# A recurrent-attention and MLP kernel on one core: a planner's order is replaced by a written one, with fewer activation-table changes and half of the transposes done by DMA

## The chip, the cores and the metric

The kernel runs on one core of a Trainium2 chip. The metric is the device time of one execution in microseconds (us); of several runs the median counts. A profile gives the span, from the first to the last instruction of one execution, and what each engine did in it: PE (TensorE matmuls; PEld its weight loads), DVE (VectorE), ACT (ScalarE), POOL (GpSimd), SP (SyncE, here only an issuer of DMAs).

## What is computed

A gated linear recurrence over 768 steps for 4 batches and 8 heads of 48 channels, then an MLP with SiLU on all 3072 tokens:

```python
f = 1.0 / (1.0 + np.exp(-f_logit))
for t in range(S):                                        # S = 768
    state = f[:, :, t, :, None] * state + np.einsum('bhd,bhe->bhde', k[:, :, t], v[:, :, t])
    y[:, :, t] = np.einsum('bhd,bhde->bhe', q[:, :, t], state)
x = y.transpose(0, 2, 1, 3).reshape(B * S, H * D)         # 3072 x 384
h = x @ w_in                                              # 384 x 2048
return (h * (1.0 / (1.0 + np.exp(-h)))) @ w_out           # 2048 x 384
```

## The kernel before

The sequence is cut into 6 chunks of 128 steps; a chunk of one batch is a *unit*, 24 in all, and two units of the same chunk make a *pair*, 12 in all. A unit passes these steps, named as in the code:

- Loads of `f`, `k`, `q`, `v` from HBM by SP (L381), in rows of 48 floats (192 bytes). Units 0 to 3 are loaded singly (192 KB per tensor), the others in pairs (384 KB).
- ACT: `E` (L388) and `L` (L390) make log(1 + exp(-f)). PE: `cs` (L431, L435) sums it over the steps. ACT: `ia` (L438) and `a` (L440) are exp of the sum and of its negative, `al` (L442) the decay over the chunk.
- POOL: `ki` = k x `ia` (L444), `vb` = v in bf16 (L446). DVE: `qg` = q x `a` (L448). Both products lie in one tile, `qk`.
- PE: `tq` transposes `qk` in eight matmuls against an identity (L454); DVE: `qkc` copies the result out of PSUM as `qkT` (L456).
- PE: `sc` = scores (L465); DVE: `at` masks them (L469). PE: `y` (L474 with the state of the chunk before, L478 within the chunk). DVE: `yc` copies y to bf16 (L482). PE: `yT` transposes it (L486); DVE: `xc` copies it into `xT` (L488).
- PE: `d` (L494), DVE: `sd` (L499, L501) and POOL: `su` (L505) carry the state on to the next chunk.

A pair then passes the MLP: eight `mi` (L412, six matmuls of 256 columns each), each followed on ACT by `si`, SiLU (L408); for each unit four `mo` (L422, four matmuls of 384 columns each); DVE: `oc` (L425) copies the result out, and `so` (L428) stores it, on POOL's queue but for the last two units. `wi` (L400) and `wo` (L403) load the MLP's weights in four parts each, on POOL's queue.

The order is made by a planner inside the kernel: `make_tasks` gives each step an engine, a duration and a rank, `schedule` plays them against numbers of buffers (`SLOTS`) and a model of the two DMA queues, and the tasks are emitted in order of their planned start. Every engine runs its own instructions in exactly that order. On ACT the planner knows two modes, `exp` for E, L, `ia`, `a`, `al` and `silu` for `si`, and adds 1.29 us where the mode turns. The code names one activation table at the start only:

```python
nc.scalar.preload_act_table_set("natural_log_exp_and_others")
```

PSUM is divided by use: `mlp` three banks, `sc` two, `tq` (for `tq` and `yT`), `cs` and `yd` (for `y` and `d`) one each. `CFG["turned"]` says from which unit on `qk` is transposed by a DMA (`qkD`) in place of `tq` and `qkc`; it is 24, so no unit is.

Of the kernel before, what the change touches and what calls it, by code (L numbers as in the profile page):

```python
# [18 lines left out]
CHUNKS, BATCHES = 6, 4  # L19
UNITS = CHUNKS * BATCHES  # L20
PAIRS = UNITS // 2
NTILES = 16

CFG = dict(
    margin=0.35,
    pace=4.43,
    turned=24,
    dma_rate=187.0,
    w_after=(2, 2, 2, 2, 2, 2, 2, 4),
    hold_exp=0.28,  # L30
    hold_silu=0.58,
    keep_exp=166.39,
    keep_silu=46.33,
    rank=dict(ld=-19.78, E=-11.45, cs=-8.27, ia=-3.88, ki=-66.76, vb=-27.12, qg=6.22, tq=-14.46, qkc=71.64,
              sc=-51.69, at=-136.35, y=-13.92, yc=-24.21, yT=-146.22, xc=36.71, d=5.82, sd=-59.94, su=-32.83,
              mi=-43.24, si=-2.57, mo=11.89, mstep=0.05, oc=38.35, so=-26.29, wi=-16.05, wo=-11.92),
)
# [4 lines left out]
LAT = {"PE": 0.25, "ACT": 0.14, "DVE": 0.14, "POOL": 0.08, "SP": 0.0}  # L42
TABLE = 1.29

class Task:
    def __init__(self, name, eng, dur, prio, deps=(), acq=(), use=(), mode=None, phase=None, load=0.0):
        self.name, self.eng, self.dur, self.prio = name, eng, dur, prio
        self.deps, self.acq, self.use = list(deps), list(acq), list(use)
        self.mode, self.phase, self.load = mode, phase, load  # L50

class Inst:
    def __init__(self, key, cls):
        self.key, self.cls = key, cls

def make_tasks(cfg):
    T, tasks, pace, R = {}, [], cfg["pace"], cfg["rank"]

    def add(name, *a, **k):
        t = Task(name, *a, **k)
        T[name] = t
        tasks.append(t)
        return t

    kb = lambda n: n * 1024.0 / (cfg["dma_rate"] * 1e3)
    I = {}

    def inst(key, cls):  # L70
        if key not in I:
            I[key] = Inst(key, cls)
        return I[key]

    base = lambda u: pace * u
    for P in range(PAIRS):
        u0 = 2 * P
        for n, x in enumerate("fkqv"):
            inst((x, P), x)
        groups = [(u0,), (u0 + 1,)] if P < 2 else [(u0, u0 + 1)]  # L80
        for us in groups:
            for n, x in enumerate("fkqv"):
                add((x, us), "SP", 0.35 * len(us), base(us[0]) + R['ld'] + n * 0.1, acq=[I[x, P]], load=kb(192 * len(us)))
    load_of = lambda x, u: T[x, (u,)] if u < 4 else T[x, (u - u % 2, u - u % 2 + 1)]

    for P in range(PAIRS):
        us_list = [(2 * P,), (2 * P + 1,)] if P < 2 else [(2 * P, 2 * P + 1)]
        for us in us_list:
            n = len(us)
            ph = us[0] // 2 - 1 if us[0] >= 4 else 0  # L90
            e = add(("E", us), "ACT", 0.067 + 0.32 * n, base(us[0]) + R['E'], deps=[T["f", us]], acq=[inst(("e", us), "e")],
                    use=[I["f", P]], mode="exp", phase=ph)
            add(("L", us), "ACT", 0.067 + 0.32 * n, base(us[0]) + R['E'] + 0.1, deps=[e], acq=[inst(("lf", P), "lf")],
                use=[I["e", us]], mode="exp", phase=ph)
    log_of = lambda u: T["L", (u,)] if u < 4 else T["L", (u - u % 2, u - u % 2 + 1)]

    for u in range(UNITS):
        c, b, P, B = u // BATCHES, u % BATCHES, u // 2, base(u)
        last, ph = c == CHUNKS - 1, u // 2
        dmat = u >= cfg["turned"]  # L100
        for key in ("cs", "ia", "qk", "vb", "qkT", "atm", "yb", "sc", "al"):
            inst((key, u), key)
        inst(("y", u), "yd"), inst(("d", u), "yd"), inst(("tq", u), "tq"), inst(("yT", u), "tq")
        inst(("sd", u), "sd"), inst(("st", u), f"st{b}"), inst(("xT", P), "xT"), inst(("hT", P), "hT")
        cs = add(("cs", u), "PE", 0.162 + (0 if last else 0.1), B + R["cs"], deps=[log_of(u)], acq=[I["cs", u]], use=[I["lf", P]])
        ia = add(("ia", u), "ACT", 0.387, B + R["ia"], deps=[cs], acq=[I["ia", u]], use=[I["cs", u]], mode="exp", phase=ph)
        a = add(("a", u), "ACT", 0.38, B + R["ia"] + 0.1, deps=[ia], use=[I["cs", u]], mode="exp", phase=ph)
        if not last:
            al = add(("al", u), "ACT", 0.19, B + R["ia"] + 0.2, deps=[cs], acq=[I["al", u]], use=[I["cs", u]], mode="exp", phase=ph)
        ki = add(("ki", u), "POOL", 1.02, B + R["ki"], deps=[ia, load_of("k", u)], acq=[I["qk", u]], use=[I["ia", u], I["k", P]])  # L110
        vb = add(("vb", u), "POOL", 0.62, B + R["vb"], deps=[load_of("v", u)], acq=[I["vb", u]], use=[I["v", P]])
        qg = add(("qg", u), "DVE", 0.45, B + R["qg"], deps=[a, load_of("q", u)], acq=[I["qk", u]], use=[I["cs", u], I["q", P]])
        if dmat:
            qkT = add(("qkD", u), "SP", 2.3, B + R["tq"], deps=[qg, ki], acq=[I["qkT", u]], use=[I["qk", u]], load=0.5)
        else:
            tq = add(("tq", u), "PE", 0.45, B + R["tq"], deps=[qg, ki], acq=[I["tq", u]], use=[I["qk", u]])
            qkT = add(("qkc", u), "DVE", 0.6, B + R["qkc"], deps=[tq], acq=[I["qkT", u]], use=[I["tq", u]])
        sc = add(("sc", u), "PE", 0.41, B + R["sc"], deps=[qkT], acq=[I["sc", u]], use=[I["qkT", u]])
        at = add(("at", u), "DVE", 1.21, B + R["at"], deps=[sc], acq=[I["atm", u]], use=[I["sc", u]])
        yd = [at, vb] + ([T["su", u - BATCHES]] if c else [])  # L120
        y = add(("y", u), "PE", 0.39 if c else 0.22, B + R["y"], deps=yd, acq=[I["y", u]],
                use=[I["atm", u], I["vb", u], I["qkT", u]] + ([I["st", u - BATCHES]] if c else []))
        yc = add(("yc", u), "DVE", 0.47, B + R["yc"], deps=[y], acq=[I["yb", u]], use=[I["y", u]])
        yT = add(("yT", u), "PE", 0.17, B + R["yT"], deps=[yc], acq=[I["yT", u]], use=[I["yb", u]])
        xc = add(("xc", u), "DVE", 0.3, B + R["xc"], deps=[yT], acq=[I["xT", P]], use=[I["yT", u]])
        if not last:
            d = add(("d", u), "PE", 0.17, B + R["d"], deps=[ki, vb, y], acq=[I["d", u]], use=[I["qk", u], I["vb", u]])
            sdd = [d] + ([T["su", u - BATCHES]] if c else [])
            sd = add(("sd", u), "DVE", 0.47, B + R["sd"], deps=sdd, acq=[I["sd", u]],
                     use=[I["d", u]] + ([I["st", u - BATCHES]] if c else []))  # L130
            add(("su", u), "POOL", 0.75, B + R["su"], deps=[sd, al], acq=[I["st", u]], use=[I["sd", u], I["al", u]])

    for n in range(4):
        add(("wi", n), "POOL", 0.8, R["wi"] + n, deps=[T["ki", cfg["w_after"][n]]], load=786.432e3 / 341e3)
    for n in range(4):
        add(("wo", n), "POOL", 0.8, R["wo"] + n, deps=[T["ki", cfg["w_after"][4 + n]]], load=786.432e3 / 341e3)

    for P in range(PAIRS):
        B = base(2 * P + 1)
        for j in range(NTILES // 2):  # L140
            h = inst(("h", P, j), "mlp")
            mi = add(("mi", P, j), "PE", 0.655, B + R["mi"] + j * R["mstep"], deps=[T["xc", 2 * P], T["xc", 2 * P + 1], T["wi", j // 2]],
                     acq=[h], use=[I["xT", P]])
            add(("si", P, j), "ACT", 0.504, B + R["si"] + j * R["mstep"], deps=[mi], acq=[I["hT", P]], use=[h], mode="silu")
        for i in range(2):
            u = 2 * P + i
            o = inst(("o", u), "mlp")
            for m in range(4):
                mo = add(("mo", u, m), "PE", 0.655, B + R["mo"] + (4 * i + m) * R["mstep"],
                         deps=[T["si", P, 2 * m], T["si", P, 2 * m + 1], T["wo", m]] + ([T["mo", u, m - 1]] if m else []),  # L150
                         acq=[o], use=[I["hT", P]])
# [7 lines left out]
def schedule(tasks, slots, cfg, margin=0.0, fixed=None, dur=None):  # L159

    for i, t in enumerate(tasks):
        t.idx, t.start, t.end, t.succ, t.ready, t.left = i, None, None, [], 0.0, len(t.deps)
# [394 lines left out]
```

## Time and profile before

| what | value |
|---|---|
| three runs | 218.91, 221.58, 223.65 us; median 221.58 |
| span of the profiled execution | 217.2 us |
| profiled execution's own time | not listed apart from the three runs; the median is 4.4 us over the span |
| PE, ACT, DVE, POOL busy | 181.0, 149.4, 102.7, 75.0 us |
| mean granted clock of PE | 0.976 |
| DMA | 27.02 MB, 124 GB/s mean; 99,712 of 104,628 packets under 512 bytes |
| activation-table loads on ACT | 38 of 1283 ns |

The page cuts the span into 40 slices of 5.43 us; a digit is the busy share of an engine in tenths, PEclk the clock that PE was granted, GB/s what the DMA engines moved. A group row gives the line, engine, operation, tiles and shapes, the count, the busy time, the mean of one in ns, and the idle time ahead of them with what ended most of it. A stage row gives the stage, its length, and the busy time of PE, PEld, DVE, ACT and POOL with counts, then clock, DMA share (above 1 where transfers overlap) and GB/s. A wait row gives who waited for whom, the total, how often, and the longest. A timeline row gives start, duration, engine, line, operation, tiles and count; SPq rows are SP's queue issuing DMAs. PE's busy time is modelled for pipelined matmuls, so a busy PE need not be a dense one.

The DMA row `GB/s` of the first five slices is 121, 164, 163, 169, 196. DMA issues take, from issue to landing, a median of 5.2 to 5.3 us for 192 KB loads, 7.7 to 8.1 for 384 KB loads, 9.2 (shortest 5.8) for a part of `w_in`, 12.0 (shortest 7.5) for a part of `w_out`, 3.9 for a store from POOL and 1.9 for the last two from SP.

### The profile page before, as it was taken

The page shows a single profiled execution, that of the slowest core. Times are in us where ns is not written, and L with a number is a line of the kernel's source. Part 1 is how long each engine was busy: PE and PEld are TensorE (multiplying, and loading weights), DVE is VectorE, ACT ScalarE, POOL GpSimd, SP SyncE. Part 2 cuts the span into 40 slices and gives each one's busy share as a digit, 9 for nine tenths or more (in the row PEclk, how much of TensorE's full clock was granted, in tenths as well). Part 3 has the DMA queues.
Part 4 walks back from the last instruction along what each step waited for, and adds up shares of the span by engine and source line. Part 5 has one row for each costly group of instructions (what it writes and reads, how often), then busy time and mean ns, then how long its engine had stood idle before and what let it go on. Part 6 is the DMA issues. An engine that isn't in the chain of part 4 may idle for free.

```text
span 217.2 us, 4591 instructions
## 1 busy us (share of the span) xinstructions
PE 181.0 (83%) x1872; PEld 135.4 (62%) x1872; DVE 102.7 (47%) x201; ACT 149.4 (69%) x230; POOL 75.0 (35%) x126
## 2 busy tenths in 40 slices
PE   0366889945999966969969969986999999999992
PEld 0344668624578646648748738754769677786761
DVE  3277730027455526545545446444585573745111
ACT  4444249965079899995999995999845658662440
POOL 2248830042274146144343335235253321510100
PEclk9999999995699999999999999999999999999999
DMA  7999999999999999999999999011001010100101
GB/s 121 164 163 169 196 188 184 178 164 187 174 223 220 164 200 167 197 194 177 179 194 180 163 191 185 4 38 38 3 36 39 0 39 36 39 36 3 41 31 72
DMA packets 104628, 27.02 MB, mean 124 GB/s; under 512 B 99712, under 2 KB 103552, under 8 KB 104608
## 3 DMA queue, kind: packets, MB, share of 16 engines
q1 hardware_dynamic: 99488, 19.27, 70.1%
q0 software_dynamic: 5120, 7.47, 15.1%
q8 instruction: 14, 0.23, 0.5%
q14 instruction: 6, 0.05, 0.1%
HBM read 25.17 MB, written 4.72 MB: 138 GB/s over the span
## 4 chain that ended last, share of the span: by engine, by line
PE 62%; ACT 19%; DMA 6%; SPq 5%; issue 3%; DVE 2%; POOL 0%; DVEq 0%; ACTq 0%; POOLq 0%
PE mlp L412 27%; PE mlp L422 21%; SPq L381 5%; ACT L438 4%; DMA w_out_sb<-in_moe_w_out_dram 3%; PE tq L454 3%; ACT lf L390 3%; PE sc L465 3%; ACT L390 3%; DMA f<-in_f_logit_dram 2%; ACT e L388 2%; ACT L388 2%; ACT ia L438 2%; PE yd L478 2%; PE cs L431 2%
## 5 line engine op out<-in xcount | busy, mean ns | idle before, releaser
L408 ACT ACTIVATE hT<-mlp 128x512 bf16<-128x512 f32 x96 | 56.1, 597 | 28.6 <-PE mlp L412 25.0
L422 PE MATMUL mlp<-w_out_sb,hT 128*128 128x384 bf16 x384 | 71.5, 331 | 2.6 <-DMA w_out_sb<-in_moe_w_out_dram 2.6
L412 PE MATMUL mlp<-xT,w_in_sb 128*128 128x256 bf16 x576 | 68.8, 276 | 3.3 <-DVE o L425 1.7
L412 PEld LDWEIGHTS <-w_in_sb 128*128 128x128 bf16 x576 | 55.8, 99 | 11.5 <-issue 3.6
L422 PEld LDWEIGHTS <-hT 128*128 128x128 bf16 x384 | 35.6, 99 | 23.0 <-issue 3.6
L469 DVE TENSOR_TENSOR atm<-sc,triu 128x512 bf16<-128x512 f32 x48 | 30.9, 685 | 31.0 <-PE sc L465 30.9
L444 POOL TENSOR_TENSOR qk<-k,ia 128x384 bf16<-128x384 f32 x24 | 23.9, 996 | 58.5 <-ACT ia L438 50.4
L448 DVE TENSOR_TENSOR qk<-q,cs 128x384 bf16<-128x384 f32 x24 | 13.2, 550 | 37.5 <-ACT al L442 36.3
L428 POOL DMA_DIRECT2D out_dram<-o x22 | 12.7, 576 | 41.6 <-DVE o L425 36.7
L505 POOL TENSOR_TENSOR st<-sd,al 48x192 bf16<-48x192 f32 x40 | 20.0, 500 | 19.4 <-DVE sd L499 8.2
L438 ACT ACT_TABLE_LOAD x14 | 18.0, 1283 | 9.2 <-PE cs L435 8.6
L454 PE MATMUL tq<-ident,qk 128*128 128x128 bf16 x192 | 16.8, 238 | 8.9 <-DVE xT L488 6.2
L456 DVE COPY qkT<-tq 128x1024 bf16<-128x1024 bf16 x24 | 16.5, 687 | 8.5 <-PE tq L454 8.5
L425 DVE COPY o<-mlp 128x384 f32<-128x384 f32 x24 | 13.2, 552 | 15.0 <-PE mlp L422 14.9
L454 PEld LDWEIGHTS <-qk 128*128 128x128 bf16 x192 | 13.2, 106 | 11.2 <-issue 6.9
L438 ACT ACTIVATE ia<-cs 128x384 f32<-128x384 f32 x24 | 11.7, 490 | 11.6 <-PE cs L435 7.5
L431 PE MATMUL cs<-lf,triu 128*128 128x384 bf16 x24 | 8.4, 350 | 13.2 <-ACT lf L390 7.9
L482 DVE CAST yb<-yd 128x384 bf16<-128x384 f32 x24 | 13.3, 554 | 10.9 <-PE yd L478 10.7
L388 ACT ACTIVATE e<-f 128x768 f32<-128x768 f32 (+1 forms) x14 | 10.5, 748 | 8.0 <-DMA f<-in_f_logit_dram 8.0
L446 POOL CAST vb<-v 128x384 bf16<-128x384 f32 x24 | 11.7, 503 | 10.5 <-issue 5.0
L435 PEld LDWEIGHTS <-lf 128*128 128x128 bf16 x80 | 5.1, 100 | 15.1 <-issue 13.8
L408 ACT ACT_TABLE_LOAD x10 | 12.8, 1283 | 0.2
(35 smaller groups left out, 154.3 us busy)
## 6 DMA issues: line engine op xcount, KB each, us to landing
out_dram<-o POOLq DMA_DIRECT2D x22, 192.0 KB, 3.9
f<-in_f_logit_dram SPq DMA_DIRECT2D x10, 384.0 KB, 8.1
k<-in_k_dram SPq DMA_DIRECT2D x10, 384.0 KB, 7.7
q<-in_q_dram SPq DMA_DIRECT2D x10, 384.0 KB, 7.9
v<-in_v_dram SPq DMA_DIRECT2D x10, 384.0 KB, 7.8
w_in_sb<-in_moe_w_in_dram POOLq DMA_DIRECT2D x4, 384.0 KB, 9.2
w_out_sb<-in_moe_w_out_dram POOLq DMA_DIRECT2D x4, 384.0 KB, 12.0
f<-in_f_logit_dram SPq DMA_DIRECT2D x4, 192.0 KB, 5.2
```

The lines of the kernel that those rows point to most:

```text
L388: nc.scalar.activation(e, at("f", u // 2)[:, i:i + n, :, 0:D], AF.Exp, scale=-1.0)
L408: return nc.scalar.activation(at("hT", P)[:, 2 * j:2 * j + 2, :], h, AF.Silu)
L412: nc.tensor.matmul(h[:, i, :], w_in_sb[:, kk, n * 128:(n + 1) * 128], at("xT", P)[:, kk, :], start=(kk == 0), stop=(kk == KT - 1))
L422: nc.tensor.matmul(o, at("hT", P)[:, n, i * C:(i + 1) * C], w_out_sb[:, n, :], start=(n == 0), stop=(n == NT - 1))
L425: nc.vector.tensor_copy(at("ob", u), at("o", u)[:, 0:d_model])
L438: nc.scalar.activation(at("ia", u).rearrange("p h d -> p (h d)"), at("cs", u)[:, 0:HD], AF.Exp)
L444: nc.gpsimd.tensor_mul(at("qk", u)[:, 1, :, 0:D], at("k", P)[:, i, :, 0:D], at("ia", u))
L454: nc.tensor.transpose(t_ps[:, j, p, :], at("qk", u)[:, j, 2 * p:2 * p + 2, :], ident)
L456: nc.vector.tensor_copy(at("qkT", u), at("tq", u).rearrange("p (j n c) -> p j n c", j=2, c=C))
L469: nc.vector.tensor_mul(at("atm", u)[:, r], at("sc", u)[:, r], triu[:, None, :].to_broadcast([C, NP, C]))
L482: nc.vector.tensor_copy(at("yb", u), at("y", u))
L505: nc.gpsimd.tensor_mul(at("st", u)[lo:lo + D, :, r * D:(r + 1) * D], at("sd", u)[lo:lo + D, :, r * D:(r + 1) * D], at("al", u)[lo:lo + D, ...
```

## The change

The planner goes. `PLAN` is a text with one word for each step, in order: name, pair and unit, engine (P, A, V, G for POOL, S for SP) and buffers. `run` reads a word and calls `emit`, which issues nearly the same instructions as before. What differs:

The built order of ACT has 18 table loads: one at the start and 17 turns. Before it has 38.
- **PSUM.** All eight banks are one pool `pb`, used by `cs`, `tq`, `sc` (two banks), `y`, `yT`, `d`, `h` and `o` as the plan says. `a` goes to a tile in SBUF, no longer in place into `cs`.
- **Turned by DMA.** For pairs 6 to 11 (12 units) `qkD` transposes `qk` straight into `qkT` and `yD` transposes `yb` straight into `xT`, both issued by SP; `tq`, `qkc`, `yT` and `xc` remain for pairs 0 to 5.
- **Idle matmuls.** 79 matmuls of 512 columns (and two of 128) with zeros as data stand in PE's order, in twelve groups, nearly all ahead of the first `mi`.
- **Other engines.** ACT takes 13 `yc`, 13 `oc`, 5 `vb`, 4 `xc`, 4 `sd`, 3 `qkc`; DVE takes 7 `ki` and 7 `vb`; POOL takes 10 `qg`. 11 of 24 stores go through SP.
- **Loads.** `f` comes in 384 KB per pair, `k`, `q`, `v` in 192 KB per unit, each at a place of its own in SP's order. The numbers of buffers change (`f` 4, `v` 6, `vb` 7, `atm` 4, `ob` 6).
- The 16 `mi` of pairs 0 and 1 are split into halves of 128 columns, one for each unit.

`emit` also holds another form of pair ("T"), which no pair uses.

```diff
-SLOTS = dict(f=5, k=6, q=6, v=5, e=2, lf=3, ia=2, qk=5, vb=6, qkT=4, atm=3, yb=3, xT=4, hT=4, sd=2, al=6, o=3,
-             st0=1, st1=1, st2=1, st3=1, mlp=3, sc=1, tq=1, cs=1, yd=1)
+SLOTS = dict(f=4, k=6, q=6, v=6, e=2, lf=3, x=5, qk=5, vb=7, qkT=4, atm=4, yb=3, xT=4, hT=4, sd=2, al=6, ob=6, pb=8, st0=1, st1=1, st2=1, st3=1)
...
+PLAN = """
+f.0.0:S:0 f.1.0:S:1 f.2.0:S:2 E.0.0:A:0 L.0.0:A:0 v.1.1:S:0 idle.512.23::7 cs.0.1:P:0 k.1.1:S:0 cs.0.0:P:1 ia.0.1:A:0 E.1.0:A:1 k.0.1:S:1 q.0.1:S:0
...
+al.1.0:A:1 ia.0.0:A:3 qg.0.0:V:2 k.2.1:S:2 al.2.1:A:2 idle.512.1::6 sc.1.1:P:6,4 vb.1.1:A:2 ki.0.0:G: ia.2.0:A:4 at.1.1.0:V:1 al.0.1:A:3 al.2.0:A:4
+k.2.0:S: wi.0:G: ki.1.0:V:3 idle.512.3::1 tq.0.0:P:7 y.0.1:P:1 qkc.0.0:V:2 d.0.1:P:0 q.2.0:S: yc.0.1:A:0 al.1.1:A:5 at.1.1.1:V: qg.1.0:G: a.2.1:A:2
...
+mo.9.1.0:P:1 si.9.7:A: mo.9.0.0:P:4 qg.11.1:V:2 ki.11.1:V: mo.9.1.1:P: qkD.11.1:S:2 mo.9.0.1:P: oc.7.0:V:0 mi.10.0:P:6 v.11.1:S: mi.10.2:P:0
...
+        elif kind == "qkD":
+            nc.sync.dma_start_transpose(out=at("qkT", P, i).rearrange("p j n c -> p (j n) c"), in_=at("qk", P, i).rearrange("p j h d -> p (j h d)"))
...
+        elif kind == "yD":
+            nc.sync.dma_start_transpose(out=at("xT", P)[:, :, i * C:(i + 1) * C], in_=at("yb", P, i))
...
+    def run(kind, rest, eng, got):
+        if kind == "idle":
+            for _ in range(rest[1]):
+                nc.tensor.matmul(buf["pb", int(got)][:, 0:rest[0]], triu, zero[:, 0:rest[0]], start=True, stop=True, skip_group_check=True)
+            return
...
+    modes = [(n, mode_of(kind)) for n, (kind, *_) in enumerate(plan) if mode_of(kind)]
+    turns = {n: TABLES[m2] for (n, m), (_, m2) in zip(modes, modes[1:]) if m != m2}
...
-        for t in tasks:
-            if t not in first:
-                emit(t)
+        for n, t in enumerate(plan):
+            if t not in loads:
+                run(*t)
+            if n in turns:
+                nc.scalar.preload_act_table_set(turns[n])
```

More of the change, by code (lines that the diff above doesn't have):

```diff
@@ L53 @@
[L53 to L151, printed above, removed]
-            oc = add(("oc", u), "DVE", 0.47, B + R["oc"] + 4 * i, deps=[mo], acq=[inst(("ob", u), "o")], use=[o])
-            late = u >= UNITS - 2
-            add(("so", u), "SP" if late else "POOL", 0.35 if late else 0.8, B + R["so"] + 4 * i, deps=[oc], use=[I["ob", u]],
-                load=0.6)
-    return tasks, T
@@ L310 @@
-ENGINES = ("PE", "ACT", "DVE", "POOL", "SP")
-def planned(cfg, slots):
-    tasks, T = make_tasks(cfg)
-    schedule(tasks, slots, cfg, cfg["margin"])
-    return sorted(tasks, key=lambda t: (t.start, t.idx))
+PAIRS = [
+    ('N', (0, 0), (1, 0)),
+    ('N', (2, 0), (3, 0)),
+    ('N', (0, 1), (1, 1)),
+    ('N', (2, 1), (3, 1)),
+    ('N', (0, 2), (1, 2)),
+    ('N', (2, 2), (3, 2)),
+    ('N', (0, 3), (1, 3)),
+    ('N', (2, 3), (3, 3)),
+    ('N', (0, 4), (1, 4)),
+    ('N', (2, 4), (3, 4)),
+    ('N', (0, 5), (1, 5)),
+    ('N', (2, 5), (3, 5)),
+]
@@ L368 @@
     SRC = {"f": f_logit, "k": k, "q": q, "v": v}
-    tasks = planned(CFG, SLOTS)
+    plan = []
+    for word in PLAN.split():
+        name, eng, got = word.split(":")
+        kind, *rest = name.split(".")
+        plan.append((kind, tuple(int(x) for x in rest), eng, got))
+    count = {}
+    for kind, rest, eng, got in plan:
+        if kind in "fkqvEL":
+            count[kind, rest[0]] = count.get((kind, rest[0]), 0) + 1
+        elif kind in ("wi", "wo"):
+            count[kind] = count.get(kind, 0) + 1
@@ L371 @@
+    where_u = {(b, c): (P, i) for P, (kind, *us) in enumerate(PAIRS) for i, (b, c) in enumerate(us)}
     where = {}
-    for t in tasks:
-        for x in t.acq + t.use:
-            where[x.key] = buf[x.cls, x.slot]
     at = lambda *key: where[key]
-    def load(x, us):
-        u, n = us[0], len(us)
-        c, b = divmod(u, B)
-        dst = at(x, u // 2)[:, u % 2:u % 2 + n].rearrange("p b h d -> p (b h) d")[:, :, 0:D]
-        nc.sync.dma_start(out=dst, in_=SRC[x].rearrange("b h s d -> s (b h) d")[c * C:(c + 1) * C, b * H:(b + n) * H])
@@ L383, in logs @@
[L383 to L405 removed]
+    ENG = {"A": nc.scalar, "V": nc.vector, "G": nc.gpsimd, "S": nc.sync}
@@ new lines, in emit @@
+        if kind == "y" and T:
+            first = [True, True]
+            for j in range(2):
+                for h in range(H):
+                    for r in range(2):
+                        rows = slice(r * HC, (r + 1) * HC)
+                        nc.tensor.matmul(at("y", P, r)[:, D * h:D * (h + 1)], at("atm", P, j)[rows, h % 2, h // 2, :],
+                                         at("vb", P, j)[rows, h, :], start=first[r], stop=(j == 1), skip_group_check=True)
+                        first[r] = False
+            return
@@ new lines, in emit @@
+        if kind == "d" and T:
+            todo = [r for r in range(2) if us[r][1] < CHUNKS - 1]
+            for j in range(2):
+                vv = at("vb", P, j).rearrange("p (n r) d -> p n (r d)", r=2)
+                for p in range(NP):
+                    for r in todo:
+                        rows = slice(r * HC, (r + 1) * HC)
+                        d_ps = at("d", P, r)[:, 0:HD].rearrange("p (n w) -> p n w", w=2 * D)
+                        nc.tensor.matmul(d_ps[:, p, :], at("qk", P, j)[rows, 1, 2 * p:2 * p + 2, :], vv[rows, p, :],
+                                         start=(j == 0 and p == 0), stop=(j == 1), skip_group_check=True)
+            return
@@ L418, in emit @@
+        i = rest[1]
+        b, c = us[i]
         last = c == CHUNKS - 1
         if kind == "mo":
-            o = at("o", u)[:, 0:d_model]
-            for n in range(4 * rest[1], 4 * rest[1] + 4):
-                nc.tensor.matmul(o, at("hT", P)[:, n, i * C:(i + 1) * C], w_out_sb[:, n, :],
-                                 start=(n == 0), stop=(n == NT - 1))
+            o = at("o", P, i)[:, 0:d_model]
+            for n in range(4 * rest[2], 4 * rest[2] + 4):
+                nc.tensor.matmul(o, at("hT", P)[:, n, i * C:(i + 1) * C], w_out_sb[:, n, :], start=(n == 0), stop=(n == NT - 1))
@@ L476, in emit @@
                     first = False
[L477 to L480 removed]
+            if kind == "y":
+                for h in range(H):
+                    nc.tensor.matmul(y[:, D * h:D * (h + 1)], at("atm", P, i)[:, h % 2, h // 2, :], at("vb", P, i)[:, h, :],
+                                     start=first, stop=True, skip_group_check=True)
+                    first = False
@@ L508, in emit, with takes @@
         else:
             raise ValueError(kind)
+    def takes(kind, rest):
+        if kind in ("wi", "wo", "so", "yi", "idle"):
+            return []
+        P = rest[0]
+        T = PAIRS[P][0] == "T"
+        if kind in SRC:
+            return [(kind, P)]
+        if kind in ("E", "L"):
+            return [("e" if kind == "E" else "lf", P)]
+        if kind == "mi":
+            return [("h", P, rest[1])]
+        if kind in ("si", "xc", "yD"):
+            return [("hT" if kind == "si" else "xT", P)]
+        if kind == "al":
+            return [("al", *rest)]
+        if T and kind in ("y", "d"):
+            return [(kind, P, i) for i in range(2) if kind == "y" or PAIRS[P][1 + i][1] < CHUNKS - 1]
+        if kind in ("qkc", "qkD"):
+            return [("qkT", P)] if T else [("qkT", *rest)]
+        if kind == "sc":
+            return [(f"s{r}", *rest) for r in range(2)]
+        if kind == "at":
+            return [("atm", *rest[:2])]
+        if kind == "mo":
+            return [("o", *rest[:2])]
+        return [({"ki": "qk", "qg": "qk", "yc": "yb", "oc": "ob", "su": "st"}.get(kind, kind), *rest[:2])]
```

507 lines of the change are left out of this document (246 added, 261 removed).

## The prediction

> **What bounds the kernel now.** I read the busy table and the forty slices, then busy time by stage, ScalarE's timeline in a middle stage, the waits, and SP's timeline. All rows come from one execution with a span of 217.2 us. The three listed runs have a median of 221.58 us, so 4.4 us lie around that span if the execution was an ordinary one (1.7 us against the lowest run).
>
> ```profile
> PE 181.0 (83%) x1872; PEld 135.4 (62%) x1872; DVE 102.7 (47%) x201; ACT 149.4 (69%) x230; POOL 75.0 (35%) x126
> ...
> PE   0366889945999966969969969986999999999992
> ...
> ACT  4444249965079899995999995999845658662440
> ...
> PEclk9999999995699999999999999999999999999999
> DMA  7999999999999999999999999011001010100101
> ```
>
> ```profile
> 60.00:150.00 90.00, 77.45 (x863) 58.49 (x860) 45.76 (x87) 81.18 (x119) 37.28 (x63) 1.00 1.13 163
> 150.00:214.00 64.00, 62.92 (x647) 47.40 (x646) 31.65 (x59) 36.46 (x60) 16.52 (x26) 1.00 0.08 29
> ```
>
> The columns after a stage's length are PE, weight loads, DVE, ACT, POOL. To 24 us the loads bound everything. To 60 us the MLP weights arrive and PE waits on and off, once with its clock at 0.5. From 60 to 150 us ACT is busy 81.2 of 90 us and PE idles 12.5. From 150 us PE is busy 62.9 us of 63.5, so matmul prices read there are those of a dense PE.
>
> ```profile
> 70.06 1.28 ACT L388 ACT_TABLE_LOAD   x1
> 71.36 0.84 ACT L388 ACTIVATE e<-f 128x768 f32<-128x768 f32 x1
> 72.22 1.28 ACT L390 ACT_TABLE_LOAD   x1
> 73.51 0.84 ACT L390 ACTIVATE lf<-e 128x768 bf16<-128x768 f32 x1
> 74.89 1.28 ACT L438 ACT_TABLE_LOAD   x1 [0.53 <-PE cs L435]
> ```
>
> This is the waste: E, L and `ia` each bring in a table, although the planner prices E, L and `ia` as one mode. The groups by line count 14 + 10 + 10 + 3 + 1 = 38 loads, 48.8 us.
>
> ```profile
> PE mlp L422 <- DMA w_out_sb<-in_moe_w_out_dram: 2.6, 1, 2.6
> ```
>
> ```profile
> 16.70 1.14 SPq L381 DMA_DIRECT2D v<-in_v_dram  x1
> ...
> 23.29 11.42 SPq L381 DMA_DIRECT2D q<-in_q_dram  x1
> 34.76 6.59 SPq L381 DMA_DIRECT2D v<-in_v_dram  x1
> ```
>
> SP issues as fast as its queue drains: 1.14 us per 192 KB, and 11.42 us where weights take the queue.
>
> **The change part by part.** *Tables.* The new order of ACT has 17 turns and the first load, 18 in all: 20 x 1.283 = 25.7 us go. In exchange ACT takes 42 copies. The nearest rows are 128x384 activations at 490 ns: 39 x 0.49, and three 128x1024 at about 1.05 us (line through 0.52 at 384 and 0.84 at 768), 22.3 us. ACT keeps about 146 us, but no longer 90% in one stage.
>
> The Trainium skill's ScalarE: Activation LUTs, under "Table sets: the hidden batching unit", puts a switch at about 2.7 us; by it the 20 loads would be worth an estimated 54 us. The trace has 1.283 us, which decides.
>
> *DVE and POOL.* DVE loses 10 `qg`, 15 `qkc`, 13 `yc`, 16 `xc`, 13 `oc`, 4 `sd` (38 us by its rows) and takes 7 `ki` and 7 `vb` at 0.55: about 72 us. POOL loses 7 `ki`, 12 `vb`, 9 stores and takes 10 `qg` at 1.0: 67 us. Neither binds, so this costs nothing while PE covers it.
>
> *PE.* Dense prices from the chain of waits: six `mi` 0.655, four `mo` 0.65, `tq` 0.45, `sc` 0.33, `y` 0.48 (0.28 state, 0.20 rest), `d` 0.22, `yT` 0.17 (three at `tq`'s 0.056), `cs` 0.30; a half-width `mi` 0.34 (six at 0.056). New total: 80 x 0.655 + 32 x 0.34 + 96 x 0.65 + 12 x 0.45 + 24 x (0.33 + 0.48 + 0.30) + 20 x 0.22 + 12 x 0.17 = 164 us. The old order is 171.5 us: the 12 turned units save 7.4. Besides there are 79 idle 512-column matmuls at 0.216 (0.109 per 256): 17.1 us.
>
> *Opening.* Ahead of the first `mi` the order has 7.0 us of real work and 16.7 of idle matmuls. Start at 1.4 us (triu is there at 1.3). Before, the `mi` from 24.35 to 28.4 us still took 0.24 each, then 0.12: some 4 us of dense work at half speed, so +2.1. That is 27.2. The other side is data: `wi.0` is now behind `ki.0.0`, which waits for `ia.0.0`, which is behind `vb.0.1` on ACT, which waits for the twelfth load. 2.95 MB have landed at 19.4 us by the GB/s row. Then 0.5 + 0.17 + 0.49 + 1.0 + 0.8 reach 22.4, and the fastest `w_in` landing, 5.8 us, gives 28.2. First `mi` at 28.0; ends 24.3 (as before) and 31 (a median landing, 9.2). So the idle matmuls buy a warm clock, not an earlier MLP; queued ahead of `cs.0.1`, they end at 8.4 us, when its input should have lain ready for about 1.5 (192 KB in at 3.9, 192 more at 5.0, E and L at 0.84 each).
>
> *Weights.* `wo.3` follows `vb.2.1` and three `su` on POOL. The order has 21.7 us of PE work between the first `mi` and the first `mo` on it: reached at 49.7, landing at 28 + 15.8 + 0.8 + 7.5 (the last one before) = 52.1. Cost 2.4; ends 0 and 6 (landing 12.0, the median).
>
> *Loads and turns.* The `f`, `k`, `q`, `v` bytes are unchanged, and 12 q/k turns of 256 KB and 12 y turns of 96 KB join their queue. No row shows a turn. By bytes at 172 GB/s (192 KB in 1.14) they take 1.5 and 0.57 us, 24.9 in all; less than 0 is excluded, since they add transfers. At 54 us about 13 MB remain, 8.25 pairs at 10.24 (49.92 to 131.8 for eight), so the last `v` lands at 54 + 84.5 + 24.9 = 163.4. From its use 17.4 us of PE remain: that path ends at 184.5 with the tail, 13 us inside my sum. Latency is dearer. A q/k turn has 4.5 to 7.5 us of PE work between its place and its first user, a y turn 2.9 to 5.0, mean 3.8, once per pair for six pairs. Landing like SP's last stores on an empty queue (1.9 us) costs 0; like a 192 KB load in a full one (5.2), 6 x 1.4 = 8.4. SP now waits for compute ahead of each turn, which thins its queue, so I take 4, the middle.
>
> The Trainium skill's DMA: Bandwidth & Descriptors, under "Issuing engines are not separate DMA queues", says that DMAs from all issuers interleave on the same 16 engines, which speaks against moving PE's work there. No run here shows a turn beside loads. By the Trainium skill's VectorE: DVE Perf Modes ("The three transpose paths") a turn runs at about 90% of DMA bandwidth, which would leave the queue path inside the sum as well.
>
> *ACT pile-ups.* Summing each engine over stretches of 10 us of PE work, ACT exceeds PE twice, 12.8 against 10.6 (around `si.3`) and 13.1 against 10.5 (around `si.5` and `si.6`). Neighbours absorb about half: 2; ends 0 and 5.
>
> *Tail.* Last matmul to the end: 3.7 before (213.5 to 217.2), the same after.
>
> *Sum.* 28.0 + PE behind it (157.2 + 0.4 idle) + 2.4 + 4 + 2 + 3.7 = 197.7 us of span; with 4.4 around it 202 us.
>
> **The rivals.** *Dense:* no late weight, turn or pile-up: 28.0 + 157.6 + 3.7 + 4.4 = 194, and 190 if the first `mi` comes at 24.3. For it: the order was laid out with leads. Against: leads of 3 us, and a fixed order that cannot step aside. *The queue binds:* if turns take twice my price per byte, its path ends at 184.5 + 24.9 = 209.4, 214 us with the rest. For it: DMA is full to 134 us already. Against: from 134 us on it was nearly empty. *Slower than before:* y turns queue behind loads, and the in-order PE sits in front of the `mi` that needs them. Landing like a 384 KB load (7.9 us) costs 6 x 4.1 = 24.6 instead of 4: 222.6, no change; over 8.5 us it is slower by over 2%. For it: `q` sat 11.42 us in a contended queue. Against: a y turn is a quarter of such a load, and loads of 192 KB landed in 5.2. *Tables don't go:* excluded by the built order, which has 18.
>
> **How the numbers follow.** Main case, 196 to 209 us: 0.55. Dense, below 196: 0.17. Queue or turns partly late, 209 to 217: 0.13; up to 226: 0.07. Slower rival, beyond: 0.08. A 2% change, 4.4 us, is about what measurement can tell, so faster is below 217.1: 0.85; same 0.07; slower 0.08. The range 190 to 216 drops about 0.05 below and 0.15 above; the main case alone is 196 to 209.
>
> **What would show it.** Right: 18 table loads; ACT below 85% between 60 and 150 us; PE dense from about 28 us to 4 us before the end; no second dip of the clock; SP's last load near 160. Wrong: PE waits on `xT` or `qkT` with a DMA as releaser, over 8 us in all; turns landing over 7 us; the first `mi` beyond 31 us; E or `qg` waiting for loads after 60 us.

## The result, and the profile after

The changed kernel takes 192.91 us, the median of four runs (192.88 to 193.78); the kernel before, run beside it, 221.28 (218.91 to 223.65): 28.4 us are gone. The ratio is 0.877, with a 95% interval of 0.870 to 0.884; it is not 192.91/221.28 = 0.872, because it leaves out runs more than 1.5% above the fastest of their kernel, as do the times given below for the kernel before beside each experiment. The profiled execution took 192.9 us with a span of 191.1, so 1.8 us lie around the span.

The busy table and the slices of the page of the kernel after (columns as in the page before):

```profile
PE 182.5 (95%) x1917; PEld 132.3 (69%) x1917; DVE 77.9 (41%) x145; ACT 133.4 (70%) x248; POOL 68.2 (36%) x108
...
PE   7999886999999999999999999999999999999992
...
PEclk9999998899999999999999999999999999999999
DMA  6999899999999998101799499978899686944043
```

PE is at 9 from the eighth slice to the last but one, where it went up and down before. The clock dips once, in the seventh and eighth slices.

The stages of the kernel after (length; busy PE, weight loads, DVE, ACT, POOL; clock, DMA share, GB/s); the cuts are the first `mi`, 60 and 150 us, and the last matmul:

```profile
0.00:28.30 28.30, 25.39 (x206) 12.83 (x207) 11.59 (x28) 14.23 (x30) 8.98 (x17) 1.00 1.02 187
28.30:60.00 31.70, 29.93 (x381) 24.09 (x382) 9.57 (x18) 21.17 (x40) 12.38 (x19) 0.95 1.16 200
60.00:150.00 90.00, 89.49 (x992) 68.14 (x990) 46.91 (x83) 76.90 (x141) 37.10 (x56) 1.00 0.79 156
150.00:188.00 38.00, 37.70 (x343) 27.27 (x340) 9.88 (x18) 20.81 (x41) 9.75 (x17) 1.00 0.54 140
188.00:191.10 3.10, 0.00 (x0) 0.00 (x0) 0.00 (x0) 0.26 (x1) 0.00 (x0) 1.00 0.35 127
```

In the stage from 60 to 150 us PE idles 0.5 us where it idled 12.5, and ACT is down from 81.2 to 76.9 us although it does 141 instructions instead of 119. This row says that ACT no longer bounds the middle. The group of table loads at the turns (the eighteenth is the one at the start):

```profile
L479 ACT ACT_TABLE_LOAD x17 | 21.8, 1283 | 0.3
```

PE's waits of the kernel after (who waited for whom; total, times, longest), the whole list down to 0.3 us:

```profile
PE pb L248 <- ACT xT L184: 1.6, 1, 1.6
PE pb L428 <- POOL triu masks.py:66: 1.4, 1, 1.4
PE pb L323 <- DVE qk L316: 0.9, 1, 0.9
PE pb L377 <- POOL vb L186: 0.5, 1, 0.5
PE pb L368 <- DVE yb L186: 0.3, 1, 0.3
```

Only 1.6 and 0.5 of these stand behind the first `mi`. No load of a unit, no weight and no turn holds PE up for more than 0.3 us. The turns, in the page's DMA issues (median us from issue to landing at the end):

```profile
qkT<-qk SPq DMA_TRANSPOSE x12, 3.4
xT<-yb SPq DMA_TRANSPOSE x12, 2.6
```

### The profile page after: what moved, and what is told of

It is laid out like the page before. It is cut to its first block, busy times and chain, and to the rows that moved or that the text cites. A ratio compares the mean times of both kernels' runs of the same rounds, so it can differ in the third digit from the quotient of the medians.

```text
span 191.1 us, 4704 instructions
## 1 busy us (share of the span) xinstructions
PE 182.5 (95%) x1917; PEld 132.3 (69%) x1917; DVE 77.9 (41%) x145; ACT 133.4 (70%) x248; POOL 68.2 (36%) x108
## 4 chain that ended last, share of the span: by engine, by line
PE 88%; ACT 3%; DMA 3%; DVE 2%; issue 1%; POOL 1%; SPq 1%; POOLq 0%; ACTq 0%
PE pb L283 32%; PE pb L248 31%; PE pb L428 9%; PE pb L344 3%; PE pb L323 3%; DMA k<-in_k_dram 3%; PE pb L360 2%; PE pb L377 2%; PE pb L306 2%; PE pb L356 2%; PE pb L368 1%; PE pb L309 1%; DVE qkT L186 1%; ACT L479 1%; POOL qk L316 1%
## 5 line engine op out<-in xcount | busy, mean ns | idle before, releaser
L248 PE MATMUL pb<-xT,w_in_sb 128*128 128x256 bf16 (+1 forms) x672 | 71.3, 260 | 1.8 <-ACT xT L184 1.6
L253 ACT ACTIVATE hT<-pb 128x512 bf16<-128x512 f32 x96 | 51.9, 607 | 27.3 <-PE pb L248 26.8
L283 PE MATMUL pb<-w_out_sb,hT 128*128 128x384 bf16 x384 | 70.4, 326 | 0.0
L348 DVE TENSOR_TENSOR atm<-pb,triu 128x512 bf16<-128x512 f32 x48 | 31.1, 683 | 36.6 <-PE pb L344 35.9
L316 POOL TENSOR_TENSOR qk<-k,x 128x384 bf16<-128x384 f32 x17 | 17.0, 997 | 42.2 <-ACT x L311 21.4
L311 ACT ACTIVATE x<-pb 128x384 f32<-128x384 f32 x48 | 22.1, 502 | 6.9 <-PE pb L309 3.7
L428 PE MATMUL pb<-zero,triu 128*128 128x512 bf16 (+1 forms) x81 | 20.8, 399 | 1.4 <-POOL triu masks.py:66 1.4
L316 DVE TENSOR_TENSOR qk<-q,x 128x384 bf16<-128x384 f32 x14 | 12.0, 861 | 12.1 <-DMA q<-in_q_dram 12.1
L316 POOL TENSOR_TENSOR qk<-q,x 128x384 bf16<-128x384 f32 x10 | 10.0, 1000 | 18.6 <-DMA q<-in_q_dram 10.6
L233 ACT ACTIVATE e<-f 128x768 f32<-128x768 f32 x12 | 10.1, 848 | 3.5 <-DMA f<-in_f_logit_dram 3.4
```

Of the source, the lines that this page charges most:

```text
L233: return nc.scalar.activation(e, at("f", P)[:, j * w:(j + 1) * w], AF.Exp, scale=-1.0)
L248: nc.tensor.matmul(h[:, i, cols], w_in_sb[:, kk, n * 128:(n + 1) * 128], at("xT", P)[:, kk, cols], start=(kk == 0), stop=(kk == KT - 1))
L253: return nc.scalar.activation(at("hT", P)[:, 2 * j:2 * j + 2, :], at("h", P, j).rearrange("p (n c) -> p n c", n=2), AF.Silu)
L283: nc.tensor.matmul(o, at("hT", P)[:, n, i * C:(i + 1) * C], w_out_sb[:, n, :], start=(n == 0), stop=(n == NT - 1))
L311: nc.scalar.activation(at(kind, P, i).rearrange("p h d -> p (h d)"), at("cs", P, i)[:, 0:HD], AF.Exp, scale=1.0 if kind == "ia" else -1.0)
L316: ENG[eng].tensor_mul(at("qk", P, i)[:, j, :, 0:D], heads("qk"[j], P, i), at("ia" if j else "a", P, i))
```

## The experiments

Each kernel was run four times, the kernel before beside it; "after" is the 192.91 us above. They ran in three groups, each on one chip: e1 to e4; e5 to e8; e4b, e7b, e9 and e10. The kernel before took 219.8, 219.6 and 219.0 us beside them and 221.0 beside after, so a difference between groups is good to about 2 us.

### One part alone: the named tables in the old kernel

`e1_before_tables`: the kernel before, its order untouched, with the table named behind the last step of the old mode.

```diff
+            if id(t) in turn:      # the mode of the next step on ACT differs
+                nc.scalar.preload_act_table_set(TABLES[turn[id(t)]])
```

> The kernel before with its order, buffers and engines unchanged; only the activation table is named behind each turn of mode, as in the changed kernel: 20 table loads instead of 38. Theory (tables held ScalarE, and ScalarE held the stage from 60 to 150 us): ScalarE loses 18 x 1.283 = 23.1 us, PE's 12.5 us of idle time in that stage mostly go, and the time falls by 8 to 13 us, to 208 to 213. Rival (the order and the PSUM pools held that stage, the tables only filled waits): less than 3 us.

Measured: 202.86 us (202.53 to 203.25), ratio 0.921 [0.913, 0.930], 16.9 us under the 219.8 of the kernel before. Stages and table loads of this kernel:

```profile
60.00:150.00 90.00, 90.00 (x1033) 69.52 (x1032) 55.37 (x105) 72.47 (x119) 41.18 (x69) 1.00 1.13 164
...
150.00:200.70 50.70, 46.90 (x458) 34.97 (x456) 20.82 (x40) 25.72 (x41) 10.40 (x17) 1.00 0.09 32
```

```profile
L531 ACT ACT_TABLE_LOAD x19 | 24.4, 1283 | 0.3
```

18 loads fewer, 23 us of ACT, and PE is never idle in the middle: 12.5 us back there. Of the 16.5 us that the span lost (217.2 to 200.7), the rest is 1.0 less idle time between 24.4 and 60 us (28.87 to 29.87 us busy of 35.6), 0.5 in the tail, and 2.4 less busy time (181.0 to 178.6), where the clock between 24.4 and 60 us rose from 0.86 to 0.90. The theory had the mechanism; its 208 to 213 was too cautious. Naming the tables alone gives 16.9 of the 26.9 us between 219.8 and after.

### The change without its tables

`e2_after_auto_tables`: the kernel after without the loads at the turns, so that every function brings in its own (34 loads).

```diff
-            if n in turns:
-                nc.scalar.preload_act_table_set(turns[n])
```

> The changed kernel without the named loads at the turns: 34 table loads instead of 18, all else equal. Theory: 16 x 1.283 = 20.5 us come back on ScalarE, whose 133 us leave 58 free in all but little between 60 and 120 us, so PE is held up again and the time grows by 5 to 12 us. Rival (PE covers them, since more PSUM banks lie between the two engines): under 2 us.

Measured: 206.0 us (205.75 to 208.0), ratio 0.938 [0.924, 0.952], 13.1 over after. PE falls back to 79.70 of 90 us between 60 and 150. The rival, that the new order hides the loads, falls; the theory's 12 is passed by 1.1. The named tables are worth 16.9 us in the old order and 13.1 in the new, and the rest of the change 13.8 without them (219.8 to 206.0) and 10 with them (202.9 to 192.9): the two gains overlap by some 4 us. The stage from 60 to 150 us shows part of it: PE idles 12.5 us there before, none in e1, 10.3 in e2 and 0.5 after.

### The opening without idle matmuls

`e3_no_idle`: the `idle` words struck out (79 matmuls of 512 columns, two of 128), nothing else.

```diff
-... v.1.1:S:0 idle.512.23::7 cs.0.1:P:0 ... v.0.1:S: idle.512.13::7 tq.0.1:P:3 ...
+... v.1.1:S:0 cs.0.1:P:0 ... v.0.1:S: tq.0.1:P:3 ...
```

> The changed kernel without the idle matmuls (81 instructions out). Theory of the prediction (they buy a warm clock and no earlier MLP): the first MLP matmul comes at 26 to 28 us, about 4 us of it at half speed, and the time is 0 to 3 us longer. Rival one (the idle block in front of real work delays the opening): 2 to 4 us shorter. Rival two (a cold opening drags the transposes and scores too, and the clock stays down beyond it): 4 us or more longer.

Measured: 189.66 us (189.59 to 189.74), ratio 0.861 [0.854, 0.869], 3.2 us *shorter*. The theory, that they buy a warm clock and no earlier MLP, falls on its sign; rival one stands. PE's timeline, first of the kernel after, then without idle matmuls (start, duration, what; in brackets the idle time ahead of it):

```profile
13.19 2.96 PE L428 MATMUL pb<-zero,triu 128*128 128x512 bf16 x13
16.00 0.61 PE L323 MATMUL pb<-ident,qk 128*128 128x128 bf16 x8
...
28.31 0.49 PE L248 MATMUL pb<-xT,w_in_sb 128*128 128x128 bf16 x6
```

```profile
12.52 1.03 PE L323 MATMUL pb<-ident,qk 128*128 128x128 bf16 x8 [1.60 <-DVE qk L316]
...
25.36 0.49 PE L248 MATMUL pb<-xT,w_in_sb 128*128 128x128 bf16 x6 [0.21 <-DVE xT L186]
```

Without idle matmuls ahead of it `tq` takes 1.03 us instead of 0.61, a *cold* PE, although the granted clock reads 1.00 in both stretches. But it starts 3.5 us sooner, since 13 idle matmuls no longer stand in front of it. Other engines hang on it too: ACT's copy `qkc` waits for it, ACT's `ia` stands behind `qkc`, and POOL's `ki` and then `wi.0` behind `ia`. ACT and POOL of the kernel after:

```profile
16.64 1.01 ACT L184 COPY qkT<-pb 128x1024 bf16<-128x1024 bf16 x1 [4.09 <-PE pb L323]
```

```profile
18.12 1.00 POOL L316 TENSOR_TENSOR qk<-k,x 128x384 bf16<-128x384 f32 x1 [6.12 <-ACT x L311]
...
21.07 0.92 POOL L206 DMA_DIRECT2D w_in_sb<-in_moe_w_in_dram  x1
```

Up to the first `mi` the kernel after has PE busy for 25.39 us, most of it idle matmuls, and waiting for 2.8; without them PE waits for data instead, `wi.0` goes out at 18.26 us instead of 21.07 and lands at 24.9 instead of 28.0, and the first `mi` runs at 25.36 instead of 28.31. That is the 3 us. The Trainium skill's TensorE: Matmul & The Clock Gate, under "Part 1: The HAM clock gate (the "warmup" mystery)", says that about 3.4 us of sustained work bring the full clock. The trace agrees: the 23 matmuls of the first idle block take 6.66 us where 0.216 each would be 5.0, so about 8 of them, an estimated 3.4 us, ran at half speed, and behind them everything is short; in `e10_fitted_idle` the 14 of its first block take 5.85 us, so nearly all of them were slow. Here the short durations are no gain: the matmuls that bring them about stand in front of ready work, and much of that work waits for data.

### A shorter opening, and the best version

`e8_short_opening`: one idle block cut from 13 to 4, `wi.0` one step ahead, before `vb.0.0` on POOL.

> The changed kernel with 9 of the 13 idle matmuls ahead of the first transpose left out, and the first part of w_in issued ahead of vb.0.0 on POOL's queue instead of behind ki.0.0. Theory (in the opening the first transpose stands ready at 12.7 us and starts at 16.0 behind idle matmuls, and all that follows hangs on it): the first MLP matmul comes 1.5 to 3 us earlier and the time falls by 1 to 3 us. Rival (the later loads and the weights set that moment): within 1 us.

Measured: 190.26 us (189.96 to 191.21), ratio 0.868 [0.861, 0.875]; first `mi` at 25.03. Within the theory: the two edits together give back 2.7 of the 3.2 us that all idle matmuls cost. The run does not separate them.

`e9_no_idle_xc`: no idle matmuls, `wi.0` ahead, and the copy `xc.0.1`, on which PE waited for ACT, on DVE.

```diff
-... vb.0.0:G:0 idle.512.9::3 tq.1.1:P:7 ... k.2.0:S: wi.0:G: ki.1.0:V:3 ... xc.0.1:A:1 ...
+... wi.0:G: vb.0.0:G:0 tq.1.1:P:7 ... k.2.0:S: ki.1.0:V:3 ... xc.0.1:V:1 ...
```

> The changed kernel without idle matmuls, with the first part of w_in issued ahead of vb.0.0, and with xc.0.1 on DVE instead of on ACT, where it stood behind the first turn's table load while PE waited 1.6 to 1.9 us for it. Theory (PE is dense behind the opening, so what the opening gains is gained in full): 1.5 to 2.5 us shorter than without idle matmuls alone (189.66), so 187 to 188. Rival (the weights' arrival sets the stage up to 45 us): within 0.7 us of 189.7.

Measured: 188.31 us (188.06 to 188.85), ratio 0.862 [0.854, 0.870]. It is the lowest time here, 4.6 us under after. It is 1.35 under `e3_no_idle`, between theory and rival, and that is no more than groups differ. The first `mi` gained only 0.2 us (25.14 instead of 25.36), although `wi.0` went out at 15.95 us and landed at 21.9, 3 us earlier than in e3: by then the weights no longer set that moment, the units' own steps do. The 1.9 us wait of an `mi` on an ACT copy of `xT` stayed. PE's and ACT's timelines there:

```profile
28.46 0.49 PE L248 MATMUL pb<-xT,w_in_sb 128*128 128x128 bf16 x6 [1.87 <-ACT xT L184]
```

```profile
26.23 1.28 ACT L479 ACT_TABLE_LOAD   x1
27.52 0.51 ACT L184 CAST vb<-v 128x384 bf16<-128x384 f32 x1
27.94 0.47 ACT L184 COPY xT<-pb 128x384 bf16<-128x384 bf16 x1
```

The copy waited for is the next one, `xc.0.0`, which stands on ACT behind a table load and a cast. Moving that one too was not tried.

`e10_fitted_idle`: as e9, with 38 idle matmuls, fitted into gaps that e3's timeline shows.

> As the run before it (w_in ahead of vb.0.0, xc.0.1 on DVE), but with 38 idle matmuls left, only as many in each gap as PE stood idle there. Theory (a warm clock shortens the opening's chain, 0.4 us a transposition, and nothing ready is held up): 0.5 to 1.5 us shorter than without any. Rival (they still stand in front of ready work, or the clock makes no difference): equal or up to 1 us longer.

Measured: 190.39 us (189.49 to 191.21), ratio 0.870 [0.863, 0.878], 2 us longer than e9. In its profile the second and third `tq` run 0.2 to 0.3 us ahead of e9's (16.86 and 19.25 us against 17.12 and 19.48), but a `q` load comes late to POOL, which holds the fourth `tq` and the first `mi` (26.88 instead of 25.14):

```profile
22.79 0.99 POOL L316 TENSOR_TENSOR qk<-q,x 128x384 bf16<-128x384 f32 x1 [4.01 <-DMA q<-in_q_dram]
```

The load came late because of its neighbour. Here it goes out at 15.86 us, just behind `wi.0` (15.80), and lands 6.9 us later; in e9 it goes out at 14.99, ahead of `wi.0` (15.95), and lands after 3.7, while the next `q` load, at 15.87, takes 6.7. In e3, where `wi.0` goes out at 18.26, both these `q` loads take 4.0 and the one at 18.96 takes 6.7. So e10 lost its time to the order of two transfers, and its theory is not decided by it. What is shown is that no version with idle matmuls was shorter than the same without.

### The transposes: PE's or the DMA's

`e4_pe_turns`: the 12 turned units get `tq`, `qkc`, `yT` and `xc` back, at the places of the DMAs.

> The changed kernel with the 12 units of pairs 6 to 11 transposed by PE again (tq and yT on PE, the copies on DVE) at the places where the DMAs stood, in PSUM banks that are free there; no turn by DMA is left. Theory (PE is dense, so the turns are worth PE's own time): 12 x (0.45 + 0.17) = 7.4 us longer, and up to 3 more where PE waits for the product just ahead, so 200 to 204 us. Rival (the DMA queue gives back what PE wins): less than 3 us longer.

Measured: 215.74 us (215.45 to 216.04), ratio 0.980 [0.971, 0.989], 22.8 over after: far more than the 7.4 us of matmuls. PE waited about twenty times, 0.2 to 0.9 us each, for a copy made just before, so the places were wrong for PE, and the run says little on the DMA. `e4b_pe_turns_later` moves each `tq` and `yT` to the last place before its first user and into the bank that was longest free.

> As the run with the turns on PE, but each tq and yT stands later in PE's order, between its product and its first user, in the PSUM bank that is free longest around it. Theory (that run was long because PE waited in front of the moved steps and behind them for the bank, not because a turn is dear on PE): PE's added work is 7.4 us and its waits mostly go, so 199 to 204 us. Rival (the turns on PE cost about 20 us wherever they stand, through DVE and the banks): 211 us or more.

Measured: 205.63 us (205.17 to 205.93), ratio 0.940 [0.933, 0.947], 12.7 over after and 10 under e4. The span is 203.7 us with PE busy 191.1, so by the busy rows 8.6 us of the 12.6 in the span are PE work (7.4 by the prediction's sum) and 4 are new idle time. The expectation's 199 to 204 was missed by 1.6; the rival's 211 is not reached. So with these places the turns by DMA save 8.6 us of PE work, and what a still better place would give back of the other 4 was not tried.

Read behind e1, this run shows where the gain lies. Named tables: 219.8 to 202.9 us. All the rest but the turns (order, PSUM pool, other engines, loads, idle matmuls): 202.9 to 205.6, of which e3 puts some 3 on the idle matmuls. The turns: 205.6 to 192.9. Taken in this sequence the new order and its other moves bring no time of their own that exceeds the 2 us between groups; single moves, and turns by DMA in the old order, were not tried.

### What a turn costs the queue

`e7_turns_twice`: every turn is issued twice, to the same place. The output does not change.

```diff
+            for _ in range(2):
                 nc.sync.dma_start_transpose(out=at("xT", P)[:, :, i * C:(i + 1) * C], in_=at("yb", P, i))
```

> The changed kernel with each of the 24 transposing DMAs issued twice in a row to the same place (the second writes the same again), so that a consumer waits for the second: SP's time and the queue's bytes for turns double, and each turn is late by about one more. Theory (turns are hidden with room to spare): SP takes 12 x 1.28 + 12 x 1.2 = 30 us more of its idle time, PE waits little, and the time grows by 0 to 3 us. Rival (the room was just used up): 6 us or more, once per pair 1 us and up.

Measured: 265.45 us (263.73 to 266.86), ratio 1.210 [1.199, 1.221]. This kernel measures something else than meant: the second write to the same tile waits for the first to land, and SP's in-order queue waits with it. SP's waits:

```profile
SPq L332 <- DMA qkT<-qk: 32.1, 12, 5.8
SPq L374 <- DMA xT<-yb: 16.4, 12, 2.3
```

These 24 waits hold the head of the load queue for 48.5 us (2.7 in the mean for a q/k turn, 1.4 for a y turn), and PE waits 47.5 us for turns. The time grew by 72.5 us, in which the issue of 24 more turns is contained. `e7b_turns_spare` takes that wait away: the second turn of each kind goes into a spare tile that nobody reads.

```diff
+            nc.sync.dma_start_transpose(out=spare_y, in_=at("yb", P, i))
```

> The changed kernel with each transposing DMA followed by a second one of the same source into a spare tile that nobody reads, so that no consumer waits for it and SP does not wait for the first; SP's issue time and the queue's bytes for turns double. Theory (it was the wait of the second for the first, which held SP and the consumer 3 us each time, that cost 72 us; issue and bytes have room): 0 to 4 us longer than the changed kernel. Rival (turns are dear in the queue itself): 15 us or more longer.

Measured: 221.55 us (220.62 to 221.88), ratio 1.012 [1.004, 1.020], 28.6 over after. The theory (0 to 4) falls, the rival stands. The turns themselves land hardly later (3.8 and 2.9 us, after 3.4 and 2.6). What comes late is the loads. Its stages, and the issue of its last load on SP:

```profile
60.00:90.00 30.00, 30.00 (x364) 23.25 (x362) 19.89 (x36) 27.62 (x54) 15.47 (x24) 1.00 0.56 114
90.00:120.00 30.00, 26.03 (x295) 20.43 (x294) 13.66 (x22) 21.98 (x43) 10.65 (x17) 1.00 0.95 180
120.00:150.00 30.00, 25.49 (x212) 16.59 (x211) 9.45 (x17) 20.57 (x34) 5.93 (x8) 0.89 0.85 164
150.00:219.70 69.70, 57.06 (x471) 39.72 (x468) 14.75 (x26) 28.36 (x52) 15.51 (x25) 0.90 0.72 148
```

```profile
190.98 1.82 SPq L229 DMA_DIRECT2D v<-in_v_dram  x1
```

PE is dense up to 100 us, 9 us beyond the first turn (91.5), and then waits time and again. The last load is issued at 190.98 us instead of 164.67: 26.3 later, and the span is 28.6 longer. 24 more turns take about 24 x 1.3 = 31 us of SP's issuing, and they carry 4.3 MB, an estimated 25 us at 172 GB/s: these two prices lie too close together to be told apart here. PE's granted clock is also lower, 0.89 to 0.90 behind 120 us. Between the first turn and the last load SP issues for 61.0 of 74.2 us in after and for 92.3 of 101.3 here: of the 13 us in which SP waited for data the doubled turns could use 4. Transfers beyond those of the change therefore cost nearly their whole length: behind 91 us SP has little room left in this order. It stands idle just before, from 74.2 to 91.1 us, where the first turn at its head waits for its data; whether loads placed ahead of that turn would use this room was not tried.

The Trainium skill's DMA: Bandwidth & Descriptors, under "Issuing engines are not separate DMA queues", calls the time that a sequencer takes to initiate a DMA usually small beside the DMA. For these turns it is not: 1.28 us of issue (median, q/k) against 3.4 to the landing.

### Packed load tiles

One difference is not in the list of the change: the load tiles have rows of 48 floats back to back after it; before, each row had a slot of 64. `e5_padded_loads` gives them slots of 52 in the kernel after, `e6_before_packed` packs them in the kernel before.

```diff
-        f=([C, 2 * HD], F32), k=([C, 2 * HD], F32), ...
+        f=([C, 2 * H, 52], F32), k=([C, 2 * H, 52], F32), ...
```

> The changed kernel with the tiles of f, k, q and v no longer packed: each 48 floats lie in a slot of 52, so that a load writes 192-byte pieces apart from each other (the kernel before had slots of 64); bytes, order and engines equal. Theory (packed tiles are why loads of 192 KB land in 3.8 us here and 5.2 before, and why the turns found a thin queue): SP's issue in the opening goes back from about 0.9 to about 1.14 us per 192 KB, landings to about 5, and the time grows by 2 to 8 us. Rival (the loads are faster for another reason, such as their order or size): no change in issue or landing, time within 1 us.

> The kernel before with packed tiles for f, k, q and v and nothing else changed. Theory: 384 KB loads fall from 2.3 us apart to about 1.9, DMA is done near 115 us instead of 134, and the time falls by 1 to 5 us by an earlier opening and earlier weights, since the middle is bound by ScalarE. Rival: loads as before, time within 1 us.

Measured: 192.83 us (191.05 to 194.25) for e5, ratio 0.876 [0.867, 0.886], no change from after; 218.06 us (214.92 to 221.38) for e6, beside 218.29 to 223.59 for its kernel before, which leaves the difference unclear: at the same granted clock, 0.984, a run of e6 took 216.16 us and three of the kernel before 218.29 to 218.43. The DMA issues of the kernel before and of e6:

```profile
q<-in_q_dram SPq DMA_DIRECT2D x10, 384.0 KB, 7.9
...
q<-in_q_dram SPq DMA_DIRECT2D x4, 192.0 KB, 5.3
```

```profile
q<-in_q_dram SPq DMA_DIRECT2D x10, 384.0 KB, 5.7
...
q<-in_q_dram SPq DMA_DIRECT2D x4, 192.0 KB, 3.6
```

The same bytes land in 5.7 instead of 7.9 us, and 3.6 instead of 5.3. That is a real effect on the queue, and it bought little. In e6 ACT still binds the middle (PE 77.00 of 90). In e5 the landings go up, as the theory said, and the time does not, as the rival said: with slots of 52 the landings of the kernel after (4.3 to 4.6 us for 192 KB) still come in time.

## Why the prediction was right, and where it was not

It gave 202 us, 190 to 216, and faster at 0.85. The time, 192.9, lies in the range, 9 us below the middle, on the rival "dense".

- **Tables and ACT: right.** 18 loads, and the middle of PE is dense. ACT's total came to 133.4 us instead of 146. The copies did take their 0.49 us each, but neighbouring instructions overlap (four `x` of 0.50 us in 1.65, at 17.55 us), so the busy time stays under the sum; this did no harm, since ACT did not bind. The sign "ACT below 85% between 60 and 150 us" was just missed: 76.90 of 90 is 85.4%, with PE dense all the same.
- **PE's work: right.** Behind the first `mi` PE is busy 29.93 + 89.49 + 37.70 = 157.1 us; 157.6 were predicted, 0.4 of them idle matmuls. (The old order's 171.5 comes to 171.2 by the same prices; the sum does not use it.)
- **The three allowances were the failed step.** 2.4 for late weights, 4 for turns and 2 for pile-ups on ACT, 8.4 us in all, measured 2.6 (1.77 + 0.51 + 0.30 idle by the stage rows). One wait of 1.6 is of the third kind, for an ACT copy of `xT` behind a table load, though not at the `si` that the prediction names; 0.5 was for POOL's `vb`, none for a weight, 0.3 at most for a turn. That no weight was late is in part luck: the last part of `w_out` landed at 51.3 us (52.1 predicted), but PE reached its first user at 53.2 instead of 49.7, since it had waited for ACT and run at a lower clock. A `y` turn landed in a median of 2.6 us, less than the 2.9 us of PE work that stand ahead of its first user at the least by the prediction's own count; a q/k turn in 3.4, against 4.5. Loads into packed tiles, which the prediction did not see in the change, landed in 3.8 to 3.9 us instead of 5.2; but e5 shows that the time does not hang on this.
- **The time around the span was mis-sized:** 4.4 taken from the median of three runs, which was no time of the profiled execution; 1.8 measured. These 2.6, the allowances' 5.8, 0.6 in the tail (3.1 for 3.7) and 0.5 in PE's work, less 0.3 in the opening, are the whole 9.2 us between 202.1 and 192.9.
- **The opening: the number right, its reason wrong.** 28.31 against 28.0. Of the two sides worked out, PE's (27.2) and the weights' (28.2), the prediction took the weights' as the path, and the idle matmuls so for free: they "buy a warm clock, not an earlier MLP". The weights did land at 28.0, but that they and PE met there is luck: the prediction had them wait for a load, and they waited for PE's own queue, by way of `tq`, `qkc`, `ia` and `ki`. Without the idle matmuls both end 3 us earlier (e3), and with the weights 3 us earlier still the first `mi` stays at 25.1 (e9).
- **"No second dip of the clock": wrong, if it means none behind the opening.** The kernel after has clock 0.83 between 30 and 40 us in the profiled execution. It cost nothing that can be seen: another of the four runs had a mean clock of 1.000 and took 192.88 us, the profiled one 0.991 and 192.90.
- **SP's last load "near 160":** 164.67, by another way. The prediction had the queue full throughout; in the trace SP waits from 74.2 to 91.1 us for the data of the first turn, and issues for 61.0 of the 74.2 us behind it.
- **A sign of being wrong that came:** `qg` waits for loads behind 60 us, 10.6 us on POOL (5.7 at the longest) and 3.1 on DVE, and E 0.9. PE covered it, so the loads were near their limit without costing time.
- **The rival "the queue binds"** did not occur, but its mechanism lies close: it gave 214 us for turns at twice their price, and twice the turns measured 221.55. Its argument against, an empty queue from 134 us on, does not hold in the new order: DMA is busy there to 167 us.
- **The slower rival** (`y` turns landing in 7.9 us) did not occur; the longest wait for a turn is 0.3 us.

## What to carry to other kernels

Count table loads first: where an engine that paces the kernel pays 1.28 us per function change, naming the one table that holds both functions can be worth more than a new order of everything (here 16.9 of 26.9 us), for a few lines. Place nothing in an in-order engine's queue, idle work least of all, in front of a step on which another engine's chain to the first large transfer hangs. Before moving work to the DMA queue, double it into a spare place: that shows in one run how much room the queue has left in the order at hand.

## What the runs showed of the hardware

- A load of 192-byte rows lands sooner in packed rows of SBUF than in padded ones: 192 KB in 3.6 us against 5.3 (slots of 64 floats, kernel before), and 3.8 against 4.3 to 4.6 (slots of 52, kernel after).
- A transposing DMA from SBUF to SBUF takes SP 1.28 us (median) to issue for 128x1024 bf16 and 1.20 for 128x384, so hardly less for three eighths of the bytes, and lands after 3.4 and 2.6 us beside loads.
- The eight `tq` matmuls take 1.03 us on a PE that idled for much of the time before and 0.61 behind idle matmuls, while the granted clock of the profile reads 1.00 in both stretches (e3, after).
- A unit's load of 192 KB that goes out beside a part of `w_in` lands after 6.7 to 7.8 us, and after 3.7 to 4.0 ahead of it (the `q` loads of e3, e9 and e10).
